# Attention: value products of two query blocks joined into one, their transposed probabilities side by side in one buffer

## The chip, the cores and the metric

The kernel runs on one core of one Trainium2 chip. The metric is device microseconds of one execution; lower is better. Times before and after are medians of several executions, and one execution of each is profiled.

## The reference

What is computed, cut to its core (attention, then a routed expert layer, then a dense layer with a leaky activation):

```python
# q, k, v: (4, 8, 576, 64); causal by blocks of 64
scores = scale * np.matmul(q, k.transpose(0, 1, 3, 2))
scores = np.where(block_i >= block_j, scores, -1000000000.0)
attn = np.exp(scores - np.max(scores, axis=-1, keepdims=True))
attn = attn / (np.sum(attn, axis=-1, keepdims=True) + 1e-09)
x = np.matmul(attn, v)                 # to (2304, 512)
# moe: tokens with x @ w_skip > 0 go to the expert argmax(x @ w_gate)
out = x.copy(); out[do_compute] = x + gate * (relu(x @ w1[e]) @ w2[e])
# moe2
h = out @ w_in
y = (np.maximum(h, 0.0) + alpha * np.minimum(h, 0.0)) @ w_out
```

## The kernel before, in words

Three stages follow each other: attention with routing, the experts, and the dense layer. The change lies in attention; the others see it only through the time at which they start.

Attention works on 16 pairs of heads (`NPAIR`), 4 for each of 4 batches. The 64 features of the two heads lie side by side on 128 partitions. The 576 queries of a head fall into four blocks of 128 (i = 0 to 3) and a last one of 64, for which both heads together make one block of 128 rows (i = 4). Block i attends to the i + 1 key blocks up to its own. For each pair and block these steps run, in the order of blocks 4, 3, 2, 1, 0:

- `sc` (line 228): score products into a score buffer of PSUM (pool `ps_s`, 2 buffers). Lines 236 and 238 for blocks 0 to 3, line 242 for block 4.
- `row_max` (244): VectorE takes the maximum of each row (line 249).
- `expo` (257): ScalarE takes the exponential, one activation for each head, with the row sums (line 266).
- `ptr` (278): TensorE transposes the probabilities, 128x128 at a time, into PSUM buffers of the pool `ps_m` (3 buffers, shared with all other transposes): line 296, for block 4 lines 285 and 287. `copy` (272) brings them to SBUF. For blocks 2 and 3 each head has a copy of its own; which engine copies stands in `ON_ACT` (line 35): ScalarE (line 274) for blocks 0 to 3, VectorE for most of block 4 (line 276). Before the change each block has its own SBUF buffer of the tag `pt`, three of which rotate.
- `pv` (299): value products. The stationary operand is `v5[:, j, x, :]`, 64 columns of one head; the moving operand is one transposed probability tile of 128 columns; the two heads write to the two halves of the partitions of `d["o"]`, one accumulator of 512 columns for blocks 0 to 3. Block i takes i + 1 products for each head (line 315), each of which is two instructions in the trace. Behind block 0, VectorE copies the accumulator to `xt` (line 317, done at line 276).
- `norm`, `xout` (319, 332): the output is transposed back (lines 339 and 344), divided by the row sums on VectorE and written to DRAM.

A table of offsets (`OFF`, line 503) gives each step of each pair a due time, five units for a pair: scores of block n at n, its maximum at n + 0.3, exponential at n + 0.8, transposes at n + 1.7, value products at n + 2.5, where n counts the blocks in their order 4, 3, 2, 1, 0. Transposes of the next pair's queries and keys (`tr`, `tr_tail`) and `xout` have due times between. The steps are written out in the order of due times (line 554), and a planner at build time may move instructions of each engine among each other as their inputs become ready in its own estimate; what it settled is the order that each engine then follows. After the last pair's value products the order is the written one.

Routing (`route`, `weigh_all`, `route_last`, lines 367 to 401) reads the untransposed outputs `xts` of a batch, forms gate logits, and in the end scatters token lists to DRAM. The expert stage first reads these lists (line 661) and then loads large expert weights through the same load queue (SP).

Of the kernel before, what the change touches and what calls it, by code (L numbers as in the profile page):

```python
# [9 lines left out]
F32 = mybir.dt.float32  # L10
# [13 lines left out]
NP = H // 2  # L24
# [10 lines left out]
ON_ACT = ("0", "1", "2a", "2b", "3a", "3b", "5", "xt")  # L35
# [12 lines left out]
def tile_kernel(ctx: ExitStack, tc: tile.TileContext, q, k, v, w_skip, w_gate, w1, w2, w_in, w_out, alpha, out):  # L48
    nc = tc.nc
# [71 lines left out]
    ident = const.tile([128, 128], F32, name="ident")  # L121
# [14 lines left out]
    wbd = acst.tile([128, NP, 32], F32, name="wbd")  # L136
# [33 lines left out]
    ptp = ap("ptp", 3)  # L170
# [10 lines left out]
    xts = {}  # L181
# [90 lines left out]
    def copy(on_act, o, a):  # L272
        if on_act:
            nc.scalar.activation(out=o, in_=a, func=AF.Copy)  # L274
        else:
            nc.vector.tensor_copy(out=o, in_=a)

    def ptr(p, i):
        d = st[p]
        e = d.pop(("p", i))  # L280
        if i == 4:
            o = d["pt", 4] = ptp.tile([128, 5, 128], F32, tag="pt4", name="pt4", bufs=2)
            ps = ps_m.tile([128, 4, 128], F32, tag="m", name="pspt")
            for j in range(4):
                nc.tensor.transpose(ps[:, j, :], e[:, j * 128:j * 128 + 128], ident)
            p5 = ps_m.tile([64, 128], F32, tag="m", name="pspt")
            nc.tensor.transpose(p5, e[:, 512:576], ident)
            copy("4" in ON_ACT, o[:, 0:4, :], ps)
            copy("5" in ON_ACT, o[0:64, 4, :], p5)
            return  # L290
        o = d["pt", i] = ptp.tile([128, 2, i + 1, 128], F32, tag="pt", name="pt", padded_shape=[128, 2, 4, 128])
        for xs in ((0, 1),) if i < 2 else ((0,), (1,)):
            ps = ps_m.tile([128, len(xs), i + 1, 128], F32, tag="m", name="pspt")
            for y, x in enumerate(xs):
                for j in range(i + 1):
                    nc.tensor.transpose(ps[:, y, j, :], e[:, x, j * 128:j * 128 + 128], ident)  # L296
            copy((f"{i}{'ab'[xs[0]]}" if i > 1 else str(i)) in ON_ACT, o[:, xs[0]:xs[-1] + 1], ps)

    def pv(p, i):
        d = st[p]  # L300
        v5 = d["vr"]
        if i == 4:
            xts[p] = xp.tile([128, S], F32, tag="xt", name="xt")
            ps = ps_m.tile([128, 64], F32, tag="m", name="pso4")
            for j in range(5):
                kk = 128 if j < 4 else 64
                for x, hs in enumerate(half):
                    nc.tensor.matmul(ps[hs, :], v5[0:kk, j, x, :], d["pt", 4][0:kk, j, x * 64:x * 64 + 64], start=(j == 0), stop=(j == 4))
            copy("xt" in ON_ACT, xts[p][:, 512:576], ps)
            return  # L310
        if i == 3:
            d["o"] = ps_o.tile([128, 512], F32, tag="o", name="pso")
        for j in range(i + 1):
            for x, hs in enumerate(half):
                nc.tensor.matmul(d["o"][hs, i * 128:i * 128 + 128], v5[:, j, x, :], d["pt", i][:, x, j, :], start=(j == 0), stop=(j == i))  # L315
        if i == 0:
            copy("x" in ON_ACT, xts[p][:, 0:512], d["o"])

# [13 lines left out]
    def xout(p):  # L332
        d = st[p]
        b, hp = divmod(p, NP)
        r0 = b * S
        xt = xts[p]
        ps = ps_m.tile([128, 4, 2, D], F32, tag="m", name="psx")
        for t in range(4):
            nc.tensor.transpose(ps[:, t].rearrange("p h d -> p (h d)"), xt[:, t * 128:t * 128 + 128], ident)
        if hp % 2 == 0:  # L340
            xrs[p // 2] = xo.tile([128, 5, 2, 2, D], F32, tag="xr", name="xr")
        xr = xrs[p // 2][:, :, hp % 2]
        p4 = ps_m.tile([64, 2, D], F32, tag="m", name="psx")
        nc.tensor.transpose(p4.rearrange("p h d -> p (h d)"), xt[:, 512:576], ident)
        if p < NPAIR - 1:
            nc.vector.tensor_tensor(out=xr[:, 0:4], in0=ps, in1=rb[b][:, 0:4, hp, :].unsqueeze(3).to_broadcast([128, 4, 2, D]), op=ALU.mult)
            nc.vector.tensor_tensor(out=xr[0:64, 4], in0=p4, in1=rb[b][0:64, 4, hp, :].unsqueeze(2).to_broadcast([64, 2, D]), op=ALU.mult)
        else:
            for t in range(5):
                kk, src = (128, ps[:, t]) if t < 4 else (64, p4)  # L350
                for x in range(2):
                    nc.scalar.activation(out=xr[0:kk, t, x], in_=src[:, x], func=AF.Copy, scale=rb[b][0:kk, t, hp, x:x + 1])
        if p >= NPAIR - 2:
            cs = slice(hp * 128, hp * 128 + 128)
            nc.sync.dma_start(out=xd[r0:r0 + 512, cs].rearrange("(t p) d -> p t d", p=128), in_=xr[:, 0:4].rearrange("p t h d -> p t (h d)"))
            nc.sync.dma_start(out=xd[r0 + 512:r0 + S, cs], in_=xr[0:64, 4].rearrange("p h d -> p (h d)"))
            return
        if hp % 2 == 1:
            xf = xrs[p // 2].rearrange("p t a h d -> p t (a h d)")
            cs = slice((hp - 1) * 128, hp * 128 + 128)  # L360
            nc.sync.dma_start(out=xd[r0:r0 + 512, cs].rearrange("(t p) d -> p t d", p=128), in_=xf[:, 0:4])
            nc.sync.dma_start(out=xd[r0 + 512:r0 + S, cs], in_=xf[0:64, 4])
# [15 lines left out]
    def weigh(b, ps, t, kk, h0, h1):  # L378
        f = rb[b][0:kk, t, h0:h1].unsqueeze(3).to_broadcast([kk, h1 - h0, 2, 9])
        nc.vector.tensor_tensor(out=lws[b][0:kk, t, 2 * h0:2 * h1].rearrange("p (i x) c -> p i x c", x=2), in0=ps[:, :, 0:18].rearrange("p i (x c) -> p i x c", x=2), in1=f, op=ALU.mult)  # L380

    def weigh_all(b, n):
        lg = rs[b]
        ps = ps_m.tile([128, 4, NP, 32], F32, tag="m", name="psl")
        for t in range(4):
            nc.tensor.transpose(ps[:, t, 0:n].rearrange("p h c -> p (h c)"), lg[0:n * 32, t * 128:t * 128 + 128], ident[0:n * 32, 0:n * 32])
        for t in range(4):
            weigh(b, ps[:, t, 0:n], t, 128, 0, n)
        ps = ps_m.tile([64, NP, 32], F32, tag="m", name="psl")
        nc.tensor.transpose(ps[:, 0:n].rearrange("p h c -> p (h c)"), lg[0:n * 32, 512:576], ident[0:n * 32, 0:n * 32])  # L390
        weigh(b, ps[:, 0:n], 4, 64, 0, n)

    def route_last(b):
        ps = ps_m.tile([128, 5, 1, 18], F32, tag="m", name="psl")
        hp = NP - 1
        for t in range(5):
            kk = 128 if t < 4 else 64
            nc.tensor.matmul(ps[0:kk, t, 0], xts[b * NP + hp][:, t * 128:t * 128 + kk], wbd[:, hp, 0:18], start=True, stop=True)
        f = rb[b][:, 0:4, hp].unsqueeze(3).to_broadcast([128, 4, 2, 9])
        nc.vector.tensor_tensor(out=lws[b][:, 0:4, 2 * hp:2 * hp + 2], in0=ps[:, 0:4, 0].rearrange("p t (x c) -> p t x c", x=2), in1=f, op=ALU.mult)  # L400
        weigh(b, ps[0:64, 4], 4, 64, hp, NP)
# [107 lines left out]
    for p in range(NPAIR):  # L509
# [11 lines left out]
        if p % NP == NP - 1:  # L521
            b = p // NP
            last = p == NPAIR - 1
            n = NP - 1 if last else NP
# [28 lines left out]
    start = {load: WARM}  # L553
# [20 lines left out]
    ps = ps_m.tile([128, E], F32, tag="m", name="psl")  # L574
# [256 lines left out]
    xs = {}  # L831
# [175 lines left out]
    for n, (w, f) in enumerate(seq):  # L1007
        if n + 2 < len(seq):
            g1(*seq[n + 2])
        t = (f - 7) // 2  # L1010
# [43 lines left out]
```

## Time and profile before

| what | value |
|---|---|
| median of the runs | 874.42 us (874.38 to 879.89) |
| profiled execution | 874.04 us |
| its span, first to last instruction | 872.4 us |
| TensorE busy | 809.5 us (93%) |
| VectorE busy | 460.5 us (53%) |
| ScalarE busy | 302.8 us (35%) |
| mean granted TensorE clock | 0.968 of full speed |

The span is what the trace covers; the execution's time lies 1.6 us above it. Attention goes from about 22 to 256 us, routing of the last batch and the experts to about 437 us, the dense layer to the end. Engines: PE is TensorE, PEld its weight loads, DVE is VectorE, ACT is ScalarE, POOL is GpSimd, SP the engine that issues most loads. A product's end in the trace lies a fixed time behind its start, so consecutive products overlap on paper; the distance from start to start tells what one holds TensorE.

### The profile page before, as it was taken

How to read it: one execution, taken by the hardware profiler on the slowest of the kernel's cores; microseconds unless marked ns; L12 is line 12 of the kernel's file. 1: busy time of each engine (PE TensorE's matmuls, PEld its weight loads, DVE VectorE, ACT ScalarE, POOL GpSimd, SP SyncE). 2: the span in 40 equal slices, each digit the busy share in tenths (PEclk: the TensorE clock that was granted, in tenths of full speed). 3: DMA queues.
4: the chain of work that ended last, by engine and by line, in shares of the span. 5: the costliest groups of instructions: out<-in, count | busy, mean ns of one | idle time of the engine just before them, and what ended most of it. 6: DMA issues, size and time to landing. Idle time of an engine off the chain costs nothing.

```text
span 872.4 us, 15135 instructions
## 1 busy us (share of the span) xinstructions
PE 809.5 (93%) x5804; PEld 622.0 (71%) x5804; DVE 460.5 (53%) x931; ACT 302.8 (35%) x793; POOL 195.2 (22%) x225
## 2 busy tenths in 40 slices
PE   7999999999995699999489987999999999999998
PEld 4777777777763565775268765788888888888897
DVE  4565757658555566798449999322322222222232
ACT  3766666666750222212134344311121112111121
POOL 1000110110204122323025556222122221212232
PEclk7999999999998799999699999999999999999999
DMA  6664354363314777784733222100020001000000
GB/s 126 163 190 131 85 138 108 84 164 104 98 56 109 242 234 252 235 285 133 235 114 120 89 72 73 48 1 1 1 97 1 1 1 48 25 1 1 25 25 25
DMA packets 96380, 85.86 MB, mean 98 GB/s; under 512 B 68601, under 2 KB 73913, under 8 KB 96272
## 3 DMA queue, kind: packets, MB, share of 16 engines
q1 hardware_dynamic: 93776, 78.88, 30.8%
q0 software_dynamic: 2496, 5.61, 2.1%
q8 instruction: 60, 0.98, 0.4%
q14 instruction: 48, 0.39, 0.2%
HBM read 73.20 MB, written 11.71 MB: 97 GB/s over the span
## 4 chain that ended last, share of the span: by engine, by line
PE 37%; DVE 12%; DMA 9%; issue 3%; ACT 1%; POOL 1%; SPq 0%; DVEq 0%; ACTq 0%; POOLq 0%
PE psf L955 18%; PE psa L988 6%; PE psa L987 6%; PE psa L997 6%; DMA w1t<-in_moe_w_dram 3%; DMA w2t<-in_moe_w_dram 3%; DVE dt L627 2%; DVE gt L966 2%; DMA dr<-in_moe_w_in_dram 2%; DVE dr L628 1%; DVE dt L631 1%; DVE dt L630 1%; DMA dr<-in_moe_w_out_dram 1%; DVE dt L629 1%; DVE wlo L618 1%
## 5 line engine op out<-in xcount | busy, mean ns | idle before, releaser
L955 PE MATMUL psf<-xs,whi 128*128 128x512 f32 (+1 forms) x640 | 160.6, 373 | 6.1 <-ACT xs L842 6.1
L973 POOL TENSOR_TENSOR gl<-gt,gh 128x512 fp32r<-128x512 f32 (+1 forms) x72 | 85.3, 1185 | 249.3 <-PE psa L997 135.9
L955 PEld LDWEIGHTS psf<-xs,whi 128*128 128x128 f32 x640 | 114.7, 188 | 31.3 <-ACT xs L842 6.7
L972 ACT ACTIVATE gh<-gt 128x512 fp32r<-128x512 f32 (+1 forms) x80 | 47.1, 588 | 255.5 <-PE psa L988 150.0
L968 DVE TENSOR_SCALAR gu<-psf,alf 128x512 f32<-128x512 f32 (+1 forms) x64 | 43.7, 683 | 165.2 <-PE psf L955 165.0
L955 PE MATMUL psf<-xs,wlo 128*128 128x512 f32 (+1 forms) x320 | 80.6, 374 | 0.0
L266 ACT ACTIVATE pe<-pss,mx 128x512 f32<-128x512 f32 (+3 forms) x128 | 66.4, 523 | 12.0 <-DVE mx L249 10.1
L249 DVE TENSOR_REDUCE mx<-pss 128x2 f32<-128x1024 f32 (+1 forms) x64 | 52.5, 820 | 31.2 <-PE pss L238 29.3
L955 PEld LDWEIGHTS psf<-xs,wlo 128*128 128x128 f32 x320 | 57.2, 189 | 12.0
L274 ACT ACTIVATE pt<-pspt 128x512 f32<-128x512 f32 (+3 forms) x112 | 52.0, 488 | 34.3 <-PE pspt L296 33.0
L987 PE MATMUL psa<-whi,gh 128*128 128x512 f32 x144 | 57.5, 400 | 4.0 <-ACT gh L972 4.0
L315 PE MATMUL pso<-pt,vr 128*64 128x128 f32 x640 | 59.7, 285 | 0.6 <-ACT pt L274 0.5
L987 PE MATMUL psa<-wkg,gh 128*128 128x512 f32 x144 | 56.8, 394 | 1.5 <-ACT gh L972 1.5
L988 PE MATMUL psa<-wlo,gh 128*128 128x512 f32 x144 | 56.3, 391 | 0.0
L988 PE MATMUL psa<-wkg,gh 128*128 128x512 f32 x144 | 56.2, 390 | 0.0
L296 PE MATMUL pspt<-ident,pe 128*128 128x128 f32 x320 | 52.5, 286 | 0.0
L969 DVE SCALAR_TENSOR_TENSOR gt<-psf,gu 128x512 f32<-128x512 f32 (+1 forms) x64 | 40.0, 625 | 11.5 <-POOL gl L973 5.4
L315 PEld LDWEIGHTS pso<-pt,vr 128*64 128x64 f32 x640 | 39.2, 136 | 9.5 <-issue 3.1
L843 DVE TENSOR_TENSOR xs<-psx,xs 128x512 fp32r<-128x512 f32 x18 | 12.4, 690 | 56.9 <-ACT xs L842 56.9
L296 PEld LDWEIGHTS pspt<-ident,pe 128*128 128x128 f32 x320 | 34.1, 140 | 11.1 <-issue 9.6
L627 DVE TENSOR_SCALAR dt<-dr 128x512 int32<-128x512 int32 x29 | 24.3, 838 | 33.2 <-DMA dr<-in_moe_w_in_dram 28.9
L692 PE MATMUL psh<-w1t,xts 128*32 128x256 f32 x256 | 21.1, 473 | 22.0 <-DMA w1t<-in_moe_w_dram 10.5
(237 smaller groups left out, 1470.3 us busy)
## 6 DMA issues: line engine op xcount, KB each, us to landing
w1t<-in_moe_w_dram SPq DMA_DIRECT2D x32, 512.0 KB
w2t<-in_moe_w_dram SPq DMA_DIRECT2D x32, 512.0 KB
dr<-in_moe_w_in_dram SPq DMA_DIRECT2D x16, 512.0 KB
dr<-in_moe_w_out_dram SPq DMA_DIRECT2D x16, 512.0 KB
out_dram<-ob SPq DMA_DIRECT2D x18, 256.0 KB
qr<-in_q_dram SPq DMA_DIRECT2D x32, 128.0 KB
kr<-in_k_dram SPq DMA_DIRECT2D x32, 128.0 KB
vr<-in_v_dram SPq DMA_DIRECT2D x32, 128.0 KB
```

The lines of the kernel that those rows point to most:

```text
L249: nc.vector.tensor_reduce(out=m, in_=ps[:, :, 0:128 * i + 128], axis=AX.X, op=ALU.max, negate=True)
L266: ins = nc.scalar.activation(out=pt[:, x, 0:n], in_=ps[:, x, 0:n], func=AF.Exp, bias=m[:, x:x + 1], scale=1.0, accum_out=d["sum"][:, x * 4 ...
L274: nc.scalar.activation(out=o, in_=a, func=AF.Copy)
L296: nc.tensor.transpose(ps[:, y, j, :], e[:, x, j * 128:j * 128 + 128], ident)
L315: nc.tensor.matmul(d["o"][hs, i * 128:i * 128 + 128], v5[:, j, x, :], d["pt", i][:, x, j, :], start=(j == 0), stop=(j == i))
L955: nc.tensor.matmul(ps[:, 0:n], wsp[f // 4 * 4 + kk][a][:, ws], c[:, kk, 0:n], start=(n0 == 0 and kk == 0), stop=(n0 == 2 and kk == 3))
L968: nc.vector.tensor_scalar(out=u[:, 0:n], in0=ps[:, 0:n], scalar1=0.0, scalar2=alf[:, f:f + 1], op0=ALU.min, op1=ALU.mult)
L972: nc.scalar.activation(out=hi[:, 0:n], in_=t[:, 0:n], func=AF.Copy)
L973: (nc.gpsimd if w or f % 2 else nc.vector).tensor_tensor(out=lo[:, 0:n], in0=t[:, 0:n], in1=hi[:, 0:n].bitcast(F32), op=ALU.subtract)
L987: nc.tensor.matmul(o, hi[:, ts], whi, start=(f == 0), stop=False)
L988: nc.tensor.matmul(o, hi[:, ts], wlo, start=False, stop=False)
L997: nc.tensor.matmul(acc[w, t], lo[:, t * 128:t * 128 + 128], whi, start=False, stop=False)
```

## The change

The transposed probabilities of blocks 3 and 2 go to one buffer, and those of blocks 1 and 0 to another. In the buffer, key block j of the higher query block stands in slot 2j and that of the lower one in slot 2j + 1. `pv` does nothing when block 3 or block 1 is due; when block 2 or 0 is due, it does both blocks: for each key block that both attend to, one product of 256 moving columns in place of two of 128; for the last key block of the higher one, one of 128. The two buffers for blocks 3 and 2 hold 7 slots each, the single one for blocks 1 and 0 holds 3; before there were three of 4. Within a group of 512 output columns the query blocks now stand in reverse, and the readers (`xout`, `weigh_all`, `route_last`) take them from there. Copies, their engines and the due times stay.

```diff
@@ -288,13 +288,18 @@
             copy("4" in ON_ACT, o[:, 0:4, :], ps)
             copy("5" in ON_ACT, o[0:64, 4, :], p5)
             return
-        o = d["pt", i] = ptp.tile([128, 2, i + 1, 128], F32, tag="pt", name="pt", padded_shape=[128, 2, 4, 128])
+        g, first = i // 2, i % 2
+        if first:
+            n = 7 if g else 3
+            d["pt", g] = ptp.tile([128, 2, n, 128], F32, tag=f"pt{'ab'[1 - g]}", name="pt", bufs=1 + g)
+        o = d["pt", g]
         for xs in ((0, 1),) if i < 2 else ((0,), (1,)):
             ps = ps_m.tile([128, len(xs), i + 1, 128], F32, tag="m", name="pspt")
             for y, x in enumerate(xs):
                 for j in range(i + 1):
                     nc.tensor.transpose(ps[:, y, j, :], e[:, x, j * 128:j * 128 + 128], ident)
-            copy((f"{i}{'ab'[xs[0]]}" if i > 1 else str(i)) in ON_ACT, o[:, xs[0]:xs[-1] + 1], ps)
+            r = slice(1 - first, 2 * i + 2 - first, 2)
+            copy((f"{i}{'ab'[xs[0]]}" if i > 1 else str(i)) in ON_ACT, o[:, xs[0]:xs[-1] + 1, r], ps)
 
     def pv(p, i):
         d = st[p]
@@ -308,11 +313,16 @@
                     nc.tensor.matmul(ps[hs, :], v5[0:kk, j, x, :], d["pt", 4][0:kk, j, x * 64:x * 64 + 64], start=(j == 0), stop=(j == 4))
             copy("xt" in ON_ACT, xts[p][:, 512:576], ps)
             return
-        if i == 3:
+        if i % 2:
+            return
+        if i == 2:
             d["o"] = ps_o.tile([128, 512], F32, tag="o", name="pso")
-        for j in range(i + 1):
+        c0 = 256 - i * 128
+        pt = d.pop(("pt", i // 2))
+        for j in range(i + 2):
+            n = 2 if j <= i else 1
             for x, hs in enumerate(half):
-                nc.tensor.matmul(d["o"][hs, i * 128:i * 128 + 128], v5[:, j, x, :], d["pt", i][:, x, j, :], start=(j == 0), stop=(j == i))
+                nc.tensor.matmul(d["o"][hs, c0:c0 + n * 128], v5[:, j, x, :], pt[:, x, 2 * j:2 * j + n].rearrange("p n c -> p (n c)"), start=(j == 0), stop=(j == i + 1))
         if i == 0:
             copy("x" in ON_ACT, xts[p][:, 0:512], d["o"])
 
@@ -336,7 +346,7 @@
         xt = xts[p]
         ps = ps_m.tile([128, 4, 2, D], F32, tag="m", name="psx")
         for t in range(4):
-            nc.tensor.transpose(ps[:, t].rearrange("p h d -> p (h d)"), xt[:, t * 128:t * 128 + 128], ident)
+            nc.tensor.transpose(ps[:, t].rearrange("p h d -> p (h d)"), xt[:, 384 - t * 128:512 - t * 128], ident)
         if hp % 2 == 0:
             xrs[p // 2] = xo.tile([128, 5, 2, 2, D], F32, tag="xr", name="xr")
         xr = xrs[p // 2][:, :, hp % 2]
@@ -383,7 +393,7 @@
         lg = rs[b]
         ps = ps_m.tile([128, 4, NP, 32], F32, tag="m", name="psl")
         for t in range(4):
-            nc.tensor.transpose(ps[:, t, 0:n].rearrange("p h c -> p (h c)"), lg[0:n * 32, t * 128:t * 128 + 128], ident[0:n * 32, 0:n * 32])
+            nc.tensor.transpose(ps[:, t, 0:n].rearrange("p h c -> p (h c)"), lg[0:n * 32, 384 - t * 128:512 - t * 128], ident[0:n * 32, 0:n * 32])
         for t in range(4):
             weigh(b, ps[:, t, 0:n], t, 128, 0, n)
         ps = ps_m.tile([64, NP, 32], F32, tag="m", name="psl")
@@ -395,7 +405,8 @@
         hp = NP - 1
         for t in range(5):
             kk = 128 if t < 4 else 64
-            nc.tensor.matmul(ps[0:kk, t, 0], xts[b * NP + hp][:, t * 128:t * 128 + kk], wbd[:, hp, 0:18], start=True, stop=True)
+            c0 = 384 - t * 128 if t < 4 else 512
+            nc.tensor.matmul(ps[0:kk, t, 0], xts[b * NP + hp][:, c0:c0 + kk], wbd[:, hp, 0:18], start=True, stop=True)
         f = rb[b][:, 0:4, hp].unsqueeze(3).to_broadcast([128, 4, 2, 9])
         nc.vector.tensor_tensor(out=lws[b][:, 0:4, 2 * hp:2 * hp + 2], in0=ps[:, 0:4, 0].rearrange("p t (x c) -> p t x c", x=2), in1=f, op=ALU.mult)
         weigh(b, ps[0:64, 4], 4, 64, hp, NP)
```

## Rows read from the trace of the kernel before

**Rows 1.** Windows of 22 to 260 us: width; busy us (instructions); PEclk, DMA share, GB/s

```profile
22.00:100.00 78.00, 77.05 (x787) 57.88 (x787) 49.05 (x136) 53.33 (x169) 2.35 (x8) 1.00 0.56 149
100.00:200.00 100.00, 98.60 (x985) 73.94 (x980) 63.08 (x168) 66.37 (x207) 10.29 (x18) 1.00 0.48 118
200.00:260.00 60.00, 58.15 (x613) 43.15 (x613) 36.38 (x118) 38.75 (x126) 5.93 (x12) 1.00 0.30 87
```

**Rows 2.** Timeline, TensorE, one head pair: start us, us, engine, line, names, shapes, count [idle]

```profile
119.87 0.50 PE L236 MATMUL pss<-kh,qh 64*128 64x512 f32 x2
...
121.40 0.44 PE L315 MATMUL pso<-pt,vr 128*64 128x128 f32 x4
121.77 0.65 PE L285 MATMUL pspt<-ident,p 128*128 128x128 f32 x4
...
123.52 0.66 PE L339 MATMUL psx<-ident,xt 128*128 128x128 f32 x4 [0.23 <-DVE xt L276]
...
126.59 1.09 PE L296 MATMUL pspt<-ident,pe 128*128 128x128 f32 x8
...
127.76 0.30 PE L236 MATMUL pss<-kh,qh 64*128 64x128 f32 x1
127.99 0.43 PE L315 MATMUL pso<-pt,vr 128*64 128x128 f32 x2
128.36 0.33 PE L296 MATMUL pspt<-ident,pe 128*128 128x128 f32 x1
128.62 1.09 PE L315 MATMUL pso<-pt,vr 128*64 128x128 f32 x14
129.63 0.77 PE L296 MATMUL pspt<-ident,pe 128*128 128x128 f32 x5
130.33 0.32 PE L236 MATMUL pss<-kh,qh 64*128 64x128 f32 x1
...
130.85 1.12 PE L315 MATMUL pso<-pt,vr 128*64 128x128 f32 x12
131.90 0.66 PE L296 MATMUL pspt<-ident,pe 128*128 128x128 f32 x4
132.31 0.48 PE L242 MATMUL pss<-kh,qd 128*128 128x512 f32 x1
...
133.44 0.66 PE L315 MATMUL pso<-pt,vr 128*64 128x128 f32 x8
134.02 0.44 PE L296 MATMUL pspt<-ident,pe 128*128 128x128 f32 x2
134.39 0.50 PE L236 MATMUL pss<-kh,qh 64*128 64x512 f32 x2
```

**Rows 3.** Timeline, TensorE: two groups of the last pair, and line 766 of the experts

```profile
249.34 1.09 PE L315 MATMUL pso<-pt,vr 128*64 128x128 f32 x16
250.36 0.87 PE L296 MATMUL pspt<-ident,pe 128*128 128x128 f32 x6
251.17 0.33 PE L236 MATMUL pss<-kh,qh 64*128 64x128 f32 x2
...
396.53 3.67 PE L766 MATMUL psh<-w1t,xT 128*64 128x256 f32 x32
```

**Rows 4.** Timeline, VectorE: the copy of the output accumulator

```profile
122.79 0.68 DVE L276 COPY xt<-pso 128x512 f32<-128x512 f32 x1
```

**Rows 5.** Timeline, ScalarE: copies of blocks 3 and 2, exponentials of block 1 between

```profile
127.34 1.08 ACT L274 ACTIVATE pt<-pspt 128x512 f32<-128x512 f32 x2 [0.22 <-PE pspt L296]
...
128.42 0.46 ACT L266 ACTIVATE pe<-pss,mx 128x256 f32<-128x256 f32 x1
...
129.24 0.47 ACT L266 ACTIVATE pe<-pss,mx 128x256 f32<-128x256 f32 x1
...
130.17 0.87 ACT L274 ACTIVATE pt<-pspt 128x384 f32<-128x384 f32 x2 [0.25 <-PE pspt L296]
```

**Rows 6.** Timeline, load queue (SP): the first list read of the expert stage

```profile
273.13 2.26 SPq L661 DMA_DIRECT2D li<-lst  x4
```

## The prediction

> **What bounds the kernel now.** I read the page first, then the busy time by stretches, then the order of TensorE's work inside one head pair, then what ScalarE and the load queue do beside it. The change touches only the attention stage, so the stretches come first. From 22 to 260 us TensorE is busy 77.05 of 78, 98.60 of 100 and 58.15 of 60 us with the full clock granted, while VectorE and ScalarE have about a third of the time free [rows 1]. So attention is set by TensorE, and every transposition, score product and value product costs what it holds TensorE. Busy time hides short waits, because a product's end lies well after the next one's start; I therefore use differences of start times.
>
> One head pair takes 14.52 us, from the first score product of block 3 (119.87) to that of the next pair (134.39) [rows 2]. I call S, T and V of a block its scores (L236, block 4: L242), its probability transposes (L296, block 4: L285) and its value products (L315). The order in the trace is S3, V0 of the pair before, T4, S2, the output transposes (L339), S1, V4, T3, one piece of S0, V3 mixed with T2, rest of S0, V2, T1, S4 of the next pair, V1, T0 [rows 2]. That isn't source order: the planner cuts groups and fills waits. V3 is split into 2 + 14 instructions around one transpose of T2, since its second half needs a copy that is not there yet [rows 2].
>
> **The change, part by part.** V3 and V1 vanish as groups. V2 becomes V2+3, V0 becomes V0+1. Per pair, blocks 3 and 2 took 28 instructions of 128 columns, and blocks 1 and 0 took 12; afterwards the same columns come as 16 of 256 and 8 of 128.
>
> *Columns.* V1 with 8 instructions lasts 0.66 us, V3 of the last pair with 16 lasts 1.09 [rows 2, 3]: (1.09 - 0.66) / 8 = 0.054 us for one of 128 columns. The kernel already has the wide shape: L766 has 64 weight columns, 256 moving columns and the two halves in turn, 32 in 3.67 us [rows 3]. Taking off the same tail as at L315 (1.09 - 16 x 0.054 = 0.23) leaves 0.107 us each, which is twice 0.054. So a wide product costs what its columns cost, and I put the saving by width at nothing. Bounds: nothing, and 16 x 0.054 = 0.86 us a pair if the second 128 columns were free.
>
> Here a rule speaks for more. The Trainium skill (TensorE: Matmul & The Clock Gate, Back-to-back issue gap) gives 81 ns a product at 128 columns and 131 ns at 512 in a sustained stream. Read on a line between them, 256 columns would be an estimated 98 ns, and replacing two narrow ones by one wide one would save an estimated 64 ns, or 1.0 us a pair. The rows above contradict that.
>
> *Group V3 out.* From S0's first piece to its rest 2.57 us pass (127.76 to 130.33) [rows 2]. After the change only T2 stands there: in the last pair, six transposes and the step to S0 took 0.81 us (250.36 to 251.17) [rows 3], plus the step from S0's piece, 0.23 (127.76 to 127.99) [rows 2]: 1.04. That frees 1.53 us. V3's 16 instructions come back inside V2+3 as 16 x 0.054 = 0.86. Net -0.67.
>
> *Group V1 out.* From V1's first product to T0's first 0.58 us pass (133.44 to 134.02) [rows 2]. The step into T0 directly I price like that into V1, which stays. The 8 instructions come back inside V0+1 as 0.43. Net -0.15.
>
> *The wait ahead of the output transposes.* L339 waits 0.23 us for the copy of the output accumulator [rows 2], which VectorE does from 122.79 to 123.47 [rows 4]. V0+1 puts 0.43 us more work between S3 and L339, while the copy starts no later: V0 began at 121.40, and 0.43 us more ends it before the copy's 122.79. So this wait is covered: -0.23.
>
> *Copies, output order, buffers.* The copies out of PSUM move as many elements, now in strided 128-column runs into a shared buffer. Nothing in the trace shows this; the nearest is the same copy at its present spacing (two for T2 in 0.87 us) [rows 5]; I take no change, bounded by a tenth of it, 0.09 us a pair, on either side: ScalarE's cover here is its idle third [rows 1]. The reversed output columns change only addresses, and they are undone by the readers: zero. The buffers now hold two blocks and are freed later, but the next pair fills its own more than 8 us behind their last reader by the order above: zero.
>
> These sum to -0.67 - 0.15 - 0.23 = -1.05 us a pair. Of 16 pairs I count 15, the last one being drained in another order: -15.8 us is the ceiling of the mechanism as far as steps of TensorE go.
>
> *The new wait.* V3 was not only work, it was cover: it ran while T2's transposes waited and ScalarE worked on. V2+3 needs both copies of T2, and without V3 nothing but S0's rest stands between. Place them: T2 starts at 127.76 + 0.23 = 127.99 and is left at 128.80; S0's rest takes 0.52 (130.33 to 130.85) [rows 2]; TensorE asks for V2+3 at 129.32. ScalarE ends T3's copies at 127.34 + 1.08 = 128.42 and then did the first exponential of block 1 (128.42, 0.46 us), the second from 129.24, and T2's copies from 130.17 to 131.04 [rows 5]. Three cases:
> (i) T2's copies go straight behind T3's, as soon as both halves are transposed, about 128.75: done at 129.62, wait 0.30.
> (ii) One exponential goes first: the copies start between 128.88 and 129.24, in the middle 129.06, done at 129.93, wait 0.61.
> (iii) Both go first, as now: done at 131.04, wait 1.72.
> Behind V2+3 in TensorE's queue stand T1, S4 and T0, and their copies and exponentials wait with them; T1 and S4 can't be pulled ahead in (i) and (ii), because both need block 1's second exponential (S4 takes its score buffer, there are two). I take (ii): when T3's copies end at 128.42, block 1's maximum is there (its exponential did start then), while T2's first transposes are only just running; behind that one exponential, T2's copies belong to the earlier step.
>
> Sum: -1.05 + 0.61 = -0.44 us a pair, 15 times: -6.6 us. Against the profiled execution's own 874.04 us (span 872.4 us) that is 867.4 us; the median of the runs shown is 874.42, 0.4 us above it.
>
> *Is it handed on?* After attention the load queue does nothing until 273.13, when it reads back the expert lists that routing wrote; the large expert loads stand behind it [rows 6]. Routing follows the last pair, so what attention saves moves the whole remainder.
>
> **The rivals.**
> *Wait covered*, case (i): -0.75 x 15 = -11.3, 862.8 us. For it: ScalarE has time free [rows 1]. Against it: both halves of T2 must be transposed before ScalarE takes the exponential that is ready. At its end stands no wait at all, -15.8, 858.3 us, were other work placed in the hole.
> *Slower: T2's copies stay behind both exponentials*, case (iii): -1.05 + 1.72 = +0.67 a pair, +10 us, 884 us. The place is V2+3 on TensorE, the price 1.72 us a pair, and it decides from a wait of 1.05 us on. For it: this is ScalarE's order today [rows 5]. Against it: today T2 itself is late, its last five transposes starting at 129.63 behind V3 [rows 2]; they would be over 0.8 us sooner.
> *Wide products cost less per column*: 0.86 us a pair on top, 13 us, 854.5 us. Against it: L766's pace [rows 3]. The page named above would have it so; these rows don't.
> *Nothing handed on*: attention is shorter, but the loads that feed the experts end when they did: 874 us. Against it: the queue stands idle until routing's lists [rows 6].
>
> **How the numbers follow.** Forecast (ii) 0.42, from 865.5 to 870.5 by the two ends of the copies' start and the copies' own bound. Wait covered 0.29, no wait at all 0.08. Slower 0.13. Wide products cheaper 0.04. Not handed on 0.04. The forecast is 867.5 us. From 858 to 875 us the range leaves out the wide products and the slower case, 0.17. About 1%, or 8.7 us, is what a measurement here can tell from no change: faster means below 865.7. That takes the covered waits, the wide products and a sliver of the forecast: 0.44. Within 1%: the rest of the forecast, not handed on, and a slower case that stays short of 883: 0.45. Slower by over 1%: 0.11.
>
> **What would show it.** Right: the value products come 24 a pair instead of 40; two of 256 columns start about 0.215 us apart; L339 no longer waits for the copy; T3 is followed by S0 and T2 without V3; and ahead of V2+3 TensorE stands for some 0.6 us on ScalarE's copies of T2. A pair's period falls from 14.52 to about 14.1 us, and the load queue's first list read moves from 273.13 to about 266.5. Wrong: the planner moves S4 or T1 into the hole (towards 858), the period stays or grows with T2's copies behind both exponentials (towards 884), or the period falls and the list read moves but the end doesn't.

## The result and the profile after

The median fell from 875.74 to 863.52 us, five runs of each beside one another; the ratio is 0.985, with an interval from 0.981 to 0.988. That is 1.5% less. The forecast was 867.5 us in a range of 858 to 875; the gain is 12.2 us where 6.6 was forecast.

The profiled execution after the change is the slowest of its five: 870.16 us, span 868.6. Its first head pair ran at half the TensorE clock for longer than that of the kernel before; two more profiles of the same program, below, show that this varies from execution to execution. So the pairs are compared one by one, and the ends only where runs are many.

Busy time of the changed kernel from 100 to 200 us (columns as in [rows 1]):

```profile
100.00:200.00 100.00, 97.83 (x943) 72.76 (x943) 65.63 (x178) 72.05 (x224) 10.59 (x20) 1.00 0.53 130
```

TensorE is still what attention stands on: busy for 97.83 us of this stretch where it was 98.60. ScalarE rose from 66.37 to 72.05 us and VectorE from 63.08 to 65.63: the same work in less time.

TensorE's order in one plain head pair of the changed kernel (one without routing), the first row of the groups that matter, as in [rows 2]:

```profile
117.46 0.50 PE L236 MATMUL pss<-kh,qh 64*128 64x512 f32 x2
...
118.98 0.87 PE L325 MATMUL pso<-pt,vr 128*64 128x256 f32 x8
119.78 0.66 PE L285 MATMUL pspt<-ident,p 128*128 128x128 f32 x4
...
121.24 0.66 PE L349 MATMUL psx<-ident,xt 128*128 128x128 f32 x4
...
121.84 0.60 PE L201 MATMUL psk<-ident,kr 128*128 128x128 f32 x4
122.37 0.38 PE L236 MATMUL pss<-kh,qh 64*128 64x256 f32 x2
...
124.05 1.09 PE L300 MATMUL pspt<-ident,pe 128*128 128x128 f32 x8
...
125.21 0.30 PE L236 MATMUL pss<-kh,qh 64*128 64x128 f32 x1
126.36 0.32 PE L236 MATMUL pss<-kh,qh 64*128 64x128 f32 x1
...
127.18 2.11 PE L325 MATMUL pso<-pt,vr 128*64 128x256 f32 x16 [0.23 <-ACT pt L274]
129.22 0.65 PE L300 MATMUL pspt<-ident,pe 128*128 128x128 f32 x4
129.63 0.48 PE L242 MATMUL pss<-kh,qd 128*128 128x512 f32 x1
...
131.02 0.50 PE L236 MATMUL pss<-kh,qh 64*128 64x512 f32 x2
```

The period went from 14.52 to 13.56 us (117.46 to 131.02). T2 follows S0's first piece without V3 in between; L349, the old L339, no longer waits; behind it S1 runs in one piece (122.37); V0+1 and V2+3 stand where V0 and V2 stood; and V2+3 waits for ScalarE's copies. S4 runs into T0 without V1. Inside V2+3 the wide products of one head start 0.216 us apart, where the prediction had 0.215. The start-to-start times of the two pairs, with the forecast of each:

| stretch of a pair | before [rows 2] | after | forecast | measured |
|---|---|---|---|---|
| S3 to V0 | 1.53 | 1.52 | 0 | -0.01 |
| V0 (V0+1) to T4 | 0.37 | 0.80 | +0.43 | +0.43 |
| T4 to output transposes | 1.75 | 1.46 | -0.23 | -0.29 |
| output transposes to T3 | 3.07 | 2.81 | 0 | -0.26 |
| T3 to S0's first piece | 1.17 | 1.16 | 0 | -0.01 |
| S0's first piece to its rest (V3, T2) | 2.57 | 1.15 | -1.53 | -1.42 |
| S0's rest to V2 (V2+3) | 0.52 | 0.82 | +0.61 | +0.30 |
| V2 (V2+3) to T1 | 1.05 | 2.04 | +0.86 | +0.99 |
| T1 to S4 | 0.41 | 0.41 | 0 | 0 |
| S4 to S3 (V1, T0) | 2.08 | 1.39 | -0.58 | -0.69 |
| sum | 14.52 | 13.56 | -0.44 | -0.96 |

ScalarE beside it, answering [rows 5]: T3's copies, block 1's first exponential, T2's copies.

```profile
124.74 1.08 ACT L274 ACTIVATE pt<-pspt 128x512 f32<-128x512 f32 x2 [0.35 <-PE pspt L300]
...
125.81 0.46 ACT L266 ACTIVATE pe<-pss,mx 128x256 f32<-128x256 f32 x1
...
126.63 0.87 ACT L274 ACTIVATE pt<-pspt 128x384 f32<-128x384 f32 x2
```

This is the prediction's case (ii): one exponential goes between T3's copies and T2's (the other stood there too, and now comes later). The copies end at 127.50, and V2+3 begins at 127.18, when the first of the two is done: its first instructions are those of one head, and the second head waits inside the group for the second copy.

Over 14 pairs, from the second S4 to the sixteenth, before and after (the number of the line is the same):

```profile
27.95 0.48 PE L242 MATMUL pss<-kh,qd 128*128 128x512 f32 x1
...
239.38 0.48 PE L242 MATMUL pss<-kh,qd 128*128 128x512 f32 x1
```

```profile
31.36 0.48 PE L242 MATMUL pss<-kh,qd 128*128 128x512 f32 x1
...
231.17 0.48 PE L242 MATMUL pss<-kh,qd 128*128 128x512 f32 x1
```

211.43 us became 199.81: -11.6 us, or -0.83 a pair. It is less than 0.96 because of the three batch borders in this stretch, where routing is done: the two periods at each border gained 1.34 us together, where two plain ones gain 1.9.

### The profile page after: what moved, and what is told of

The parts are those of the page before. It is cut to its first block, busy times and chain, and to the rows that moved or that the text cites. A ratio compares the mean times of both kernels' runs of the same rounds, so it can differ in the third digit from the quotient of the medians.

```text
span 868.6 us, 14592 instructions
## 1 busy us (share of the span) xinstructions
PE 800.6 (92%) x5548; PEld 612.0 (70%) x5548; DVE 459.9 (53%) x931; ACT 304.4 (35%) x793; POOL 193.7 (22%) x225
## 4 chain that ended last, share of the span: by engine, by line
PE 56%; DVE 16%; DMA 15%; issue 5%; ACT 4%; SPq 1%; POOL 1%; another core or an unknown queue 1%; DVEq 0%; ACTq 0%; POOLq 0%
PE psf L966 18%; PE psa L998 6%; PE psa L999 6%; PE psa L1008 6%; DMA w1t<-in_moe_w_dram 5%; DMA w2t<-in_moe_w_dram 5%; PE pso L325 4%; PE pspt L300 4%; PE pss L236 3%; DMA dr<-in_moe_w_in_dram 3%; PE pss L242 2%; PE pso L313 2%; DVE mx L249 2%; DVE dt L638 2%; ACT pt L274 2%
## 5 line engine op out<-in xcount | busy, mean ns | idle before, releaser
L325 PE MATMUL pso<-pt,vr 128*64 128x256 f32 (+1 forms) x384 | 47.1, 356 | 3.6 <-ACT pt L274 3.6
L325 PEld LDWEIGHTS pso<-pt,vr 128*64 128x64 f32 x384 | 29.9, 138 | 17.8 <-ACT pt L274 7.8
```

What stands on the lines that cost most here:

```text
L325: nc.tensor.matmul(d["o"][hs, c0:c0 + n * 128], v5[:, j, x, :], pt[:, x, 2 * j:2 * j + n].rearrange("p n c -> p (n c)"), start=(j == 0), s ...
```

## The experiments

All nine runs are of the attention stage; each period is the distance of two S4 in plain pairs. Periods at the batch borders can move otherwise, so a period alone doesn't give the time. Ratios are to the kernel before on the same chip.

**Narrow products in the joined groups.** The joined groups stay, each product has 128 columns again, the lower block first.

```diff
-        for j in range(i + 2):
-            n = 2 if j <= i else 1
+        for m in (1, 0):
+            for j in range(i + 2 - m):
...
-                nc.tensor.matmul(d["o"][hs, c0:c0 + n * 128], v5[:, j, x, :], pt[:, x, 2 * j:2 * j + n]...
+                    nc.tensor.matmul(d["o"][hs, c0 + m * 128:c0 + m * 128 + 128], v5[:, j, x, :], pt[:, x, 2 * j + m, :], ...
```

> The joined groups stay in their places, but each product has 128 columns again: first all of the lower block, then all of the higher one. If columns cost what they cost at either width (the prediction's reading), TensorE's work per pair is the same to 0.05 us; the second of the two blocks no longer waits for its neighbour's copies product by product, so the period of a pair is 13.5 to 13.7 us (13.57 with wide products) and the time lies within 3 us of the changed kernel. If wide products are cheaper per column, up to 0.86 us a pair comes back: period 14.4 us, time about 876 us.

Ratio 0.987 (0.984 to 0.990). TensorE's timeline:

```profile
113.15 0.48 PE L242 MATMUL pss<-kh,qd 128*128 128x512 f32 x1
...
116.07 0.88 PE L325 MATMUL pso<-pt,vr 128*64 128x128 f32 x12
116.87 0.66 PE L285 MATMUL pspt<-ident,p 128*128 128x128 f32 x4
...
124.26 2.12 PE L325 MATMUL pso<-pt,vr 128*64 128x128 f32 x28 [0.23 <-ACT pt L274]
...
126.73 0.48 PE L242 MATMUL pss<-kh,qd 128*128 128x512 f32 x1
```

The period is 13.58 us (113.15 to 126.73), with wide products 13.56 to 13.57. V0+1 takes 0.80 us with 12 narrow instructions (116.07 to 116.87) and 0.80 with the changed kernel's 8, of which 4 are wide (118.98 to 119.78). Fewer instructions for the same columns save nothing. V2+3 still waits for ScalarE, since here the lower block, whose copies come last, goes first. So the wide product, which names the change, has no share in its gain.

**Only blocks 3 and 2 joined.** Blocks 1 and 0 go back to buffers and products of their own.

```diff
+        if i // 2 == 0:
+            o = d["pt", "s", i] = ptp.tile([128, 2, i + 1, 128], F32, tag=f"pt{i}", name="pt", bufs=1)
...
+        if i // 2 == 0:
+            pt = d.pop(("pt", "s", i))
+            c0 = 384 - i * 128
+            for j in range(i + 1):
+                for x, hs in enumerate(half):
+                    nc.tensor.matmul(d["o"][hs, c0:c0 + 128], v5[:, j, x, :], pt[:, x, j, :], start=(j == 0), stop=(j == i))
...
```

> Only blocks 3 and 2 are joined; blocks 1 and 0 keep their own buffers and narrow products. By the segments of the changed kernel's trace: S0's piece to its rest 2.57 to 1.15 us (-1.42), the wait ahead of V2+3 +0.30, V2+3 itself +0.99: -0.13 us a pair, period 14.4 us, about 873 us. The rival, that each group saved is worth the same: half of -0.95, period 14.05 us, about 868 us. By the prediction's own terms (-0.67 + 0.61) it is -0.06: like the first.

Ratio 0.996 (0.994 to 0.998), median 875.35 against 879.35 us. TensorE's timeline:

```profile
120.67 0.48 PE L242 MATMUL pss<-kh,qd 128*128 128x512 f32 x1
...
126.40 0.66 PE L360 MATMUL psx<-ident,xt 128*128 128x128 f32 x4 [0.22 <-DVE xt L276]
...
127.09 0.38 PE L236 MATMUL pss<-kh,qh 64*128 64x256 f32 x1
127.41 0.66 PE L201 MATMUL psk<-ident,kr 128*128 128x128 f32 x4
...
127.99 0.38 PE L236 MATMUL pss<-kh,qh 64*128 64x256 f32 x1
...
132.59 2.11 PE L336 MATMUL pso<-pt,vr 128*64 128x256 f32 x16 [0.23 <-ACT pt L274]
...
135.04 0.48 PE L242 MATMUL pss<-kh,qd 128*128 128x512 f32 x1
```

The period is 14.37 us (120.67 to 135.04): -0.15 from 14.52, as the segments said. The output transposes wait again (0.22), S1 is cut again by the keys' transposes (127.09, 127.41, 127.99), and V2+3 waits as it does in the changed kernel. This half saves V3's entry, exit and mixing with T2, which by the table is worth 0.56 us (1.42 less the 0.86 of its columns), and pays 0.43 of it back in waiting.

**Only blocks 1 and 0 joined.** The mirror image: blocks 3 and 2 keep three rotating buffers of their own.

```diff
+        if i // 2 == 1:
+            o = d["pt", "s", i] = ptp.tile([128, 2, i + 1, 128], F32, tag="pt", name="pt", padded_shape=[128, 2, 4, 128])
...
+        if i == 3:
+            d["o"] = ps_o.tile([128, 512], F32, tag="o", name="pso")
+        if i // 2 == 1:
+            pt = d.pop(("pt", "s", i))
+            c0 = 384 - i * 128
...
```

> Only blocks 1 and 0 are joined; blocks 3 and 2 keep their own buffers and narrow products. By the segments of the changed kernel's trace: S4 to S3 -0.69, V0+1 +0.43, T4 to the output transposes -0.29, these to V4 -0.26: -0.81 us a pair, period 13.7 us, 862 to 865 us. The rival of equal groups: period 14.05, about 868 us. By the prediction's own terms (-0.15 - 0.23) it is -0.38: period 14.14, about 869 us.

Ratio 0.988 (0.985 to 0.990). TensorE's timeline:

```profile
117.21 0.48 PE L242 MATMUL pss<-kh,qd 128*128 128x512 f32 x1
...
122.39 0.66 PE L360 MATMUL psx<-ident,xt 128*128 128x128 f32 x4
...
122.99 0.60 PE L201 MATMUL psk<-ident,kr 128*128 128x128 f32 x4
123.52 0.38 PE L236 MATMUL pss<-kh,qh 64*128 64x256 f32 x2
...
130.84 0.48 PE L242 MATMUL pss<-kh,qd 128*128 128x512 f32 x1
```

The period is 13.63 us (117.21 to 130.84): -0.89, nearly all of the change's gain, from a half to which the prediction's terms gave -0.38. The output transposes don't wait; the keys' transposes come right behind them (122.99), and S1 runs in one piece from 123.52. The two halves are far from equal, which puts the rival of equal groups aside.

**The joined products of blocks 3 and 2 due later**, to let other work into the hole.

```diff
-                at(s0 + n + OFF[u], fn, p, i)
+                at(s0 + n + OFF[u] + (0.6 if u == "V" and i == 2 else 0), fn, p, i)
```

> The changed kernel with the joined products of blocks 3 and 2 due 0.6 of a unit later, behind S4 of the next pair. If what is left of the hole ahead of V2+3 is a wait for T2's copies that other work can cover (0.3 us ahead of the group and about as much inside it, between its first and second head), T1 and S4 go first, the period falls from 13.57 to 13.0 us and the time by some 8 us under the changed kernel's. If T1 and S4 have to wait just as long for block 1's second exponential, the period stays within 0.2 us of 13.57 and the time within 3 us.

Ratio 0.995 (0.993 to 0.997): slower than the change. TensorE's timeline:

```profile
119.67 0.48 PE L242 MATMUL pss<-kh,qd 128*128 128x512 f32 x1
...
132.54 0.44 PE L300 MATMUL pspt<-ident,pe 128*128 128x128 f32 x2 [0.22 <-ACT pt L274]
132.91 0.65 PE L325 MATMUL pso<-pt,vr 128*64 128x256 f32 x2
133.49 0.44 PE L300 MATMUL pspt<-ident,pe 128*128 128x128 f32 x2
133.68 0.48 PE L242 MATMUL pss<-kh,qd 128*128 128x512 f32 x1
```

The period is 14.01 us (119.67 to 133.68). S4 and T1 did go ahead of most of V2+3, 14 of whose 16 instructions now start at 134.81. But the first half of T1 itself waited for ScalarE, as long behind S0's rest as V2+3 had (0.82 us), and T1 and V2+3 were each cut in two. Neither expectation held: other work went into the hole without filling it, and the later due time bought cuts.

**Block 2's copies side by side**, the second on VectorE.

```diff
-ON_ACT = ("0", "1", "2a", "2b", "3a", "3b", "5", "xt")
+ON_ACT = ("0", "1", "2a", "3a", "3b", "5", "xt")
```

> The changed kernel, with the copy of block 2's second head on VectorE in place of ScalarE, so that the two copies run side by side. If V2+3 waits for them, the wait inside the group (0.28 us) goes and the one ahead of it stays: period 13.3 us, some 4 us less. If ScalarE's copies aren't what it waits for, the period stays at 13.57. If the planner's estimate places VectorE's copy worse, other work gets in between and the period grows.

Ratio 0.984 (0.980 to 0.987). TensorE and VectorE:

```profile
115.30 0.48 PE L242 MATMUL pss<-kh,qd 128*128 128x512 f32 x1
...
126.41 1.74 PE L325 MATMUL pso<-pt,vr 128*64 128x256 f32 x16 [0.23 <-ACT pt L274]
128.08 0.66 PE L300 MATMUL pspt<-ident,pe 128*128 128x128 f32 x4
128.49 0.48 PE L242 MATMUL pss<-kh,qd 128*128 128x512 f32 x1
```

```profile
125.70 0.56 DVE L276 COPY pt<-pspt 128x384 f32<-128x384 f32 x1 [0.29 <-PE pspt L300]
```

The period is 13.19 us (115.30 to 128.49): -0.38. VectorE ends its copy at 126.26, ahead of V2+3, which now takes 1.67 us (126.41 to 128.08) instead of 2.04. So 0.37 us of the wait lay inside the group, for the second head; the part ahead of it stayed (0.23 shown). The time followed only in part: the median is 865.53 us against 866.97 for the changed kernel on the same chip, a difference within the spread, where some 4 us were expected. The trace shows why: at two of the three batch borders two periods together became 31.26 us in place of 30.43, so from the second S4 to the sixteenth only 1.4 us are gained.

**The order alone.** The kernel before with one edit in `pv`: no shared buffer, no wide product, old output order. Block 3's products wait for block 2's due time and are issued first.

```diff
-        if i == 3:
+        if i % 2:
+            return
+        if i == 2:
             d["o"] = ps_o.tile([128, 512], F32, tag="o", name="pso")
-        for j in range(i + 1):
-            for x, hs in enumerate(half):
-                nc.tensor.matmul(d["o"][hs, i * 128:i * 128 + 128], v5[:, j, x, :], d["pt", i][:, x, j, :], start=(j == 0), stop=(j == i))
+        for k in (i + 1, i):
+            for j in range(k + 1):
+                for x, hs in enumerate(half):
+                    nc.tensor.matmul(d["o"][hs, k * 128:k * 128 + 128], v5[:, j, x, :], d["pt", k][:, x, j, :], start=(j == 0), stop=(j == k))
```

> The kernel before with one edit: block 3's value products wait for block 2's due time and are issued ahead of them, block 1's wait for block 0's. Every block keeps its own buffer, every product has 128 columns, the output order is the old one. If the gain lies in the order of TensorE's groups alone, and what is left in the changed kernel is a wait for block 2's copies (0.3 us ahead of the joined group, 0.3 inside it), then block 3's 0.86 us of products cover that wait: period 13.0 us, time some 8 us under the changed kernel's, about 860 on this chip. If the shared buffer or the wide product are needed, the period lies above 13.6; if the wait isn't for block 2's copies, it stays at 13.57.

Ratio 0.981 (0.976 to 0.985). TensorE's timeline:

```profile
109.64 0.48 PE L242 MATMUL pss<-kh,qd 128*128 128x512 f32 x1
...
119.93 0.33 PE L236 MATMUL pss<-kh,qh 64*128 64x128 f32 x1
...
120.45 1.75 PE L318 MATMUL pso<-pt,vr 128*64 128x128 f32 x28
122.13 0.66 PE L296 MATMUL pspt<-ident,pe 128*128 128x128 f32 x4
122.55 0.48 PE L242 MATMUL pss<-kh,qd 128*128 128x512 f32 x1
```

The period is 12.91 us (109.64 to 122.55). S0's rest to V2+3 is 0.52 again (119.93 to 120.45), and the group takes 1.68 us, with no wait ahead of it or in it. Against the changed kernel that is 0.30 and 0.36 us less. Block 3's products need nothing of block 2 and cover its copies; a wide product over both blocks needs both from its first instruction on, so it can't. The change lies 0.66 us a pair above the order alone, and the wait ahead of V2+3 and in it accounts for that. Since this run also keeps the old buffers, it doesn't tell whether narrow products out of the shared buffer, block 3 first, would do as well.

**The changed kernel again**, beside the two above.

> The changed kernel once more, beside the others on this chip. Its period is 13.57 us again. The first pair took 19.62 us in its profiled execution and 16.66 in that of the kernel before, where TensorE ran at half its clock for 20.5 and 10.2 us; with narrow products it took 16.48 at 13.7 us. If that is chance from execution to execution, this profile may show either; if it belongs to the program, it shows 19.6 again. Time as the narrow one's on this chip, 864 to 869 us.

Ratio 0.988 (0.984 to 0.992). The first pair takes 16.24 us (S4 at 11.70 and 27.94), where the first profile had 19.6; the plain period was 13.57 in both. Windows of 20 to 31 us, after, and after again (the third value from the end is the granted clock, 1.00 being 2.4 GHz; an instant has either that or 1.2):

```profile
20.00:31.00 11.00, 11.00 (x77) 8.05 (x73) 3.48 (x9) 6.49 (x21) 0.17 (x1) 0.54 0.84 211
```

```profile
20.00:31.00 11.00, 11.00 (x100) 8.54 (x100) 5.34 (x14) 8.07 (x26) 0.17 (x1) 0.92 0.87 218
```

The same program got 0.54 of the clock from 20 to 31 us in one execution and 0.92 in another; in a third, the last run below, it got 0.93 and its first pair took 16.0 us. The long first pair belongs to the execution, not to the change.

**The order alone and the changed kernel, five rounds on one chip.**

> The order alone once more (narrow products, every block its own buffer, block 3's products issued behind S0 and ahead of block 2's), beside the changed kernel on one chip. By the periods, 12.91 against 13.57 us with three joined batch borders besides, it is 7 to 9 us shorter than the changed kernel; were the difference of the first timings chance, the two would agree within 3 us. Ratio to the kernel before 0.980.

> The changed kernel beside the order alone. Ratio to the kernel before 0.985 to 0.989, period 13.57 us; 7 to 9 us longer than the order alone.

The order alone: median 858.97 us, ratio 0.976 (0.972 to 0.980). The changed kernel: 865.95 us, ratio 0.983 (0.979 to 0.987). The kernel before: 880.49. The periods are 12.91 and 13.57 us again. The order alone is 7.0 us shorter than the change, at the low end of what was expected, and the intervals touch at their ends only; on the chip of the first timing it was 6.0 us (861.00 against 866.97). It beats both kernels with an edit of `pv` alone.

## Why the prediction was right, point by point

**The time: inside the range, but for a good part by terms that the prediction did not have.** A plain pair lost 0.96 us where 0.44 was forecast, and 863.52 us lies nearer to the rival of the covered wait (862.8) than to the forecast, though ScalarE's order is the forecast's case. The width of the range took in both. The inner bounds of the forecast don't follow from its terms either: copies that start at 128.88 or at 129.24 make waits of 0.43 and 0.79 us, and with 0.09 for the copies that is 863.4 to 871.5 us, not 865.5 to 870.5.

**TensorE's order bounds attention: right.** All that moved the period moved TensorE's groups or their waits, and the period followed the segments to 0.1 us in the two halves.

**Columns cost what they cost at 128 and at 256: right**, by the narrow products: 13.58 against 13.57 us. Without a wait inside it, V2+3 takes 1.67 us with 16 instructions (block 2's copies side by side) and 1.68 with 28 (the order alone). The rule weighed there, of the Trainium skill (TensorE: Matmul & The Clock Gate, Back-to-back issue gap), by which wide products would have been far cheaper per column, does not hold for this stream: 12 narrow instructions and 8 of both widths take the same 0.80 us.

**A group has a price of its own: right, and it is part of the mechanism; waits and cuts are the rest.** V2+3 with 28 narrow instructions takes 1.68 us when nothing waits; the prediction's 0.054 us each makes 1.51, so 0.17 is left for going from the group to the next transposes. V1 with 8 took 0.58 [rows 2], 0.15 above its columns. The Trainium skill has a rule that fits (TensorEngine Tiling (Array Packing), Key Properties): changing the tiling mode drains TensorE. The value products use the array as two halves of 64 columns, the transposes use it whole, so each group that is removed takes such changes with it. The trace agrees in the 0.15 to 0.17 us; that a drain is what passes there, no run shows.

**V3's group: 1.53 forecast, 1.42 measured. V1's: 0.58 forecast, 0.69 measured.** V1's step was undersized: S4's last product to T0 takes 0.12 us (130.54 to 130.66), where the prediction took the step into V1, 0.21 (133.23 to 133.44).

**The wait of the output transposes: right**, 0.23 forecast, 0.29 measured. **What hung on it was missed: 0.26 us a pair.** The prediction names S1 in the order without saying that it was cut, and priced the cut nowhere. In the kernel before, S1's first piece stood ahead of the keys' transposes (L201) and the rest behind them:

```profile
124.22 0.38 PE L236 MATMUL pss<-kh,qh 64*128 64x256 f32 x1
124.53 0.66 PE L201 MATMUL psk<-ident,kr 128*128 128x128 f32 x4
125.12 0.38 PE L236 MATMUL pss<-kh,qh 64*128 64x256 f32 x1
```

Where the output transposes don't wait, there is no cut. Joining blocks 1 and 0 alone removes both, joining blocks 3 and 2 alone keeps both. The kernel before itself shows it: at its three batch borders the output transposes (94.49, 155.29 and 216.09) follow without a wait, and S1 isn't cut. It also fits that the two periods of a border gain 0.57 us less than two plain ones: the wait and the cut are 0.29 and 0.26. So the two go together wherever these traces show them; that the planner cuts because of the wait in its own estimate is argued, not shown.

**The new wait: the right place, cause and case, and the right total, but counted once too often.** Ahead of V2+3 0.30 us and inside 0.36, together 0.66 against 0.61; the prediction had all of it ahead. But V2 had a wait inside it already, since it began at 130.85 and the second of T2's copies ended at 131.04 [rows 2, 5]: 12 instructions at 0.054 and 0.17 for the exit make 0.82, and it took 1.05 [rows 2]. So only 0.43 was new. Of the 0.52 us a pair between -0.44 and -0.96, this is 0.18, S1's cut is 0.26, V1's exit 0.11, the output transposes' 0.06, and V3's group gives 0.11 back.

**Handed on: right.** The first list read of the experts, answering [rows 6], in the first two profiles of the changed kernel (the third has it at 261.28):

```profile
266.62 2.42 SPq L672 DMA_DIRECT2D li<-lst  x4
```

```profile
261.27 3.22 SPq L672 DMA_DIRECT2D li<-lst  x4
```

It came 6.5 us sooner than 273.13 in the one, which had lost 3 us in its first pair, and 11.9 sooner in the other. That the first lies so close to the forecast's 266.5 is luck: a greater gain in the pairs and a longer first pair met. Over all runs the median fell by 12.2 us, as much as the 14 pairs did (11.6). Of the two profiled executions that can't be said: their spans are 868.6 and 863.5 us against 872.4, so 2.7 and 3.0 us of it were gone at the end. From the list read to the end the runs here lie from 598.9 to 603.8 us, whatever the kernel, and the kernel before's 599.3 is one execution; whether the change costs something there can't be told.

**The rivals.** Slower behind both exponentials: ScalarE's order changed as case (ii) had it. Wait covered: not in the change, but it is what the order alone does, and its -1.61 us a pair is beyond the prediction's ceiling of -1.05, for it also removes the wait inside V2 and S1's cut. The strided copies: T2's two took 0.87 us before and after [rows 5], no change.

## What to carry to other kernels

When two groups of products are merged, price what lies between groups (entry, exit, waits, cuts by other work) and leave the width of a product out until the trace shows that it is cheaper per column: here the order alone gained more than the change, and the width nothing. Ask then what the removed group covered: a product over two blocks needs both at its first instruction, while the same columns issued block by block let the earlier block cover the later one's copies. And look at what a wait displaces in a planned order; here a cut worth 0.26 us came and went with a wait of 0.23.

## What the runs showed of the hardware

The time at half clock near the start differs between executions of one program: from 20 to 31 us the granted clock was 0.54 in one profile of the changed kernel and 0.92 in another, and the first pair took 19.6 or 16.2 us (16.0 in a third). That is a spread of some 3 us in the total that no edit here explains. Two products on the two halves of 64 columns keep the same pace per column at 128 and 256 columns: 0.80 us for the same columns in 12 or 8 instructions.
